# Cross-shaped window attention on one Trainium2 core: column heads staged in padded blocks, nine more tiles off ScalarE, the first x in quarters

## The chip, the cores and the metric

The kernel runs on one core of a Trainium2 chip. The metric is device time in microseconds (us) of the whole program, as the median of several runs; the profile is of one further execution. A core has TensorE (PE, matrix products, with weight loads listed apart as PEld), VectorE (DVE), ScalarE (ACT), GpSimd (POOL) and SyncE (SP), which here only issues transfers (DMA). PE writes to PSUM, eight banks of 512 floats in each of 128 partitions; all else lies in SBUF.

## The reference

An image of 224 x 224 tokens with 96 channels goes through one projection to q, k and v. The first 48 channels attend within stripes of 8 rows, the last 48 within stripes of 8 columns; both results, side by side, go through an output projection.

```python
qkv = jnp.einsum('bhwc,cd->bhwd', x, wqkv)          # x: (1, 224, 224, 96) bf16
q, k, v = qkv[..., :C], qkv[..., C:2*C], qkv[..., 2*C:]
scale = C2 ** (-0.5)                                 # C2 = 48, sw = 8
qh = q[..., :C2].reshape(B * nh, sw * W, C2)         # 28 row stripes of 1792 tokens; kh, vh alike
ah = _softmax(einsum('bqc,bkc->bqk', qh, kh) * scale)
oh = einsum('bqk,bkc->bqc', ah, vh).reshape(B, H, W, C2)
# qv, kv, vv: q, k, v [..., C2:] regrouped to 28 column stripes of 1792 tokens
av = _softmax(einsum('bqc,bkc->bqk', qv, kv) * scale)
ov = ...                                             # regrouped back to (B, H, W, C2)
return einsum('bhwc,cd->bhwd', concat(oh, ov), wo)
```

## The kernel before, in words

**Pairs and tiles.** Stripes are worked two at a time: pairs P = 0 to 13 (`NPH` = 14) are row stripes, pairs 14 to 27 column stripes. The two stripes of a pair (w = 0, 1) fill the two halves of PE's rows. Scores are computed transposed, keys by queries; the queries come in four chunks c (512, 512, 512, 256), the keys in 14 blocks of 128. A *tile* is one key block against 512 queries for both stripes, 128 x 1024 scores in two PSUM banks (in the last chunk two key blocks of 256 queries). A pair has 14 + 14 + 14 + 7 = 49 tiles.

**Who takes the exponential.** Most tiles go to ACT: one exponential, 128 x 1024, PSUM to the buffer `PT` (L859). The rest go to DVE and POOL, which approximate the exponential with squarings. Which ones is told by `KINDS` and, per pair, `KIND_OF`: a letter for each tile of a chunk that does not go to ACT. A tile of kind P is read by DVE (`p1`, L943, to `qb`), squared, scaled and squared again by POOL (L959, L960, L956), and PE computes its scores once more (L702) so that DVE adds the final factor (`f`, L948). A tile of kind R has a second DVE step (`p2`, L945) and one square on POOL. Kind 0 and kind 2 hold eight such tiles, kind 1 nine. Then the tile meets v on PE (L715), accumulating outputs and, in a 49th column, the sum of weights.

**The order.** Every engine's instructions are laid out when the program is built. `ORDER`, one string per pair, gives PE's order by hand: q is a score pass for ACT, v a product with v, 1 and 3 the first score pass of a DVE tile (in two halves or whole), 2 and 4 its second, k a projection of the next pair (keys `K`, queries `Q`, values `V`, one `fill` each), g a piece of the output projection, f a final piece of the last pair. A planner (`Sched`, `dve_step`, `pool_step`, the times `tm`, durations such as `D_H`, due times such as `TURN`) follows this order with modelled durations and so fixes the order on DVE, POOL and SP's queue. On the chip only semaphores decide; each engine takes its instructions in the fixed order.

**Getting x in.** The first pair's x comes in four transfers of 168 KB, two on SP's queue and two on ACT's (L287, `x_lead`), into memory that later belongs to `cat`; PE turns it (L737), DVE and ACT evict. Later pairs use transfers that turn (`DMA_TRANSPOSE`, L404), and the column stripes reread turned x from DRAM (`xt_dram`, `plan_x`).

**Getting the result out.** A finished chunk is copied to `OT_sb` (L876) and turned (`turn_ot`, L414); DVE takes reciprocals of the sums (`emit_rn`), POOL multiplies (`emit_norm`, L920). In the row half the result goes through `ohn` and copies (`keep_oh`) into `cat`, which holds for every token 96 channels: 48 of the row head, 48 of the column head. In the column half POOL writes the other 48 channels into `cat` directly. Then `turn_cat` turns a pair's part of `cat` in two pieces (`oc_T`, in `oc_all`); a block of 128 turned rows holds 1 1/3 blocks of 96 channels, so `wo6` keeps six shifted copies of wo, and some blocks need two matmuls (L637). DVE evicts five blocks at a time back into `cat` (L642), in place, after the pair's turns have read it (the keys `catd`), and each block of 128 tokens x 96 channels leaves as one store of 24 KB in runs of 192 bytes. The last pair's column head is projected without a turn (`fin_fills`, L602) and added (L614).

Of the kernel before, what the change touches and what calls it, by code (L numbers as in the profile page):

```python
# [20 lines left out]
KINDS = ["PPR PPR PP ", "PPR PRR PPR ", "PPR PPR PR "]  # L21
# [11 lines left out]
D_ST, D_SW, D_TAIL = 0.64, 1.3, 0.70  # L33
XR1, XR2, TURN = 19.5, 43.0, 4.5
D_H, D_F, D_SQ, D_AF = 0.604, 1.137, 1.9, 1.03
# [4 lines left out]
NTWICE = 11  # L40


KIND_OF = [0, 1, 1, 1, 1, 1, 1, 1, 1, 1, 1, 1, 1, 1, 2, 2, 2, 2, 2, 2, 2, 2, 2, 2, 2, 2, 2, 2]
ORDER = [
    "kkkqkq3qkq3qkkqkq1qkqq1q3qvkqv2qvkqv2qvqkkvqv1qkvqvkqvv2qvqv1qvvvqvkq2vqvkqkq1qkvvq2qvv2qvvq1vqkvqvvq1vqv2qvkvqvkvq",
    "1vqvvqvq2vvq3qvvvqvv3qqvqvvqkkkq2qvqvkvqv2qkvqv2qkvvvq1qvvvvqvqvv1qvvq2vq2qvkqvvq1vqvkq2vqv2qvvq1qvvqvkqvvkqkvqvkq2vvq2qvv3",
    "qvvqv1qvvq1vqvvqvvqv1qkq1qvvvqvq2qvkkqvqvk2qvvq3qvkqvkvq4qkqv1qvvq4qvkq2vqv1qvq4vqkq2vqv1qvvqvvqv2q1qvvqvkkqq1vkv",
    "qv2qvqv1qvvvqvvqv1qq1vvqvvqvvvq4qvkvq1vqvvqvq2vqv1qvv4qkqvv1qvqvkq2vqkvvq2vkqvkq3vqkqvvvqv1qvq4vqkq3vqkvq4vqvkvq4vqkvq2vk",
    "qvvq1vqvvvvqq2vvvqvvvq2vqvq14qvqkqv3qvkvqvvqvkqv1qkqvvq1vqvkq2vqvkq2qvvvq1qv1qkqvvvqkqvvkq2qvv3qkvqv3qvvqv4qvkqv4qkqvv1",
    "qvqvvvq2vqq1vvqvv1qvvqvqv2qq4vqvkq1vqvvvqvq1vqkvkqkvvq2kqv3qkvqv4qvvqkq1vqvvvqkqvv4qvqkv2qvvq2vqv1qvq4vqvvqkvkvq1qkvvq2v",  # L50
# [5 lines left out]
    "qvvq1vqvvqvq1vqv2qvvq1vqqvvvq1qkvvqvvqkvq4vqkvq1vkqv2qvq3qkvvq2kqvvq2qvv1qvqvvqv2qkvqv3qvkqv4qkqvv1qvvqkkqvkvq2qvvq2vvv",  # L56
    "q3qvvvqvvvqv1qvq2vvvqkq1vqvvq3qvvvqvvqvkq4qkvq1vkqq2vqv4qvkqv2qvvvq1vkqvkq4vqkqv2qvvvq1qvkqvvvq2qkqvvq1vvq2qvvkqkvq1vkq",
    "1qvvqvvq1qvv2qqvvq1vvqvqvv1qvqvqkvqv2qvkqv2qvvqk2qvkqv3qvkvq3qvvvq4qvkvq2qkvqkvq1vqvqkvvqvvq2vqvvq3qvvkq4vqkvqv2qvvq1vk",
    "qvq1vqvvqvvqv1qvv2qvvq1vqq2vqkvq1qvkqvvqvkvqv1qkvvq2qkvvq4vqvvkq1qvvvqvvqkqv4qkvqv4qkvvq1qvvq1vvvqv1qvqvvvvq4qvvvkq2qkvvqkvq2",
# [114 lines left out]
def bass_standalone__window_attn_cswin__vision_kernel(  # L174
# [28 lines left out]
    with es:  # L203
# [55 lines left out]
        for b in range(2):  # L259
            for w in range(2):  # L260
                SEMS[f"x{b}{w}"] = sem(f"s_x{b}{w}")
                SEMS[f"xp{b}{w}"] = sem(f"s_xp{b}{w}")
                SEMS[f"xr{b}{w}"] = sem(f"s_xr{b}{w}")
# [896 lines left out]
        def do_q():  # L1160
# [18 lines left out]
            if P not in begun:  # L1179
                begun.add(P)  # L1180
                p_t[P] = tm["end"]
                if ph_of(P):
                    tm["sp"] = max(tm["sp"], st) + 1.5
# [173 lines left out]
```

## Time and profile before

| what | value |
|---|---|
| time, median of 3 runs | 1062.62 us (1061.92 to 1063.65) |
| profiled execution | 1062.68 us, of which the span 1060.9 us from first to last instruction |
| busy in the span | PE 1033.4, DVE 998.2, ACT 1049.3, POOL 935.5 us |
| mean granted clock of TensorE | 0.999 |
| exponential tiles on ACT; tiles on DVE and POOL | 1135; 237 |
| matmuls of the output projection (L637) | 1176 |
| stores, 24 KB each | 392 |

The span is what the trace covers; the rest of the execution's own time lies around it. In a group's row, "x1135 | 1044.8, 1087" means 1135 instructions, 1044.8 us in which at least one of them ran, and 1087 ns for one; behind the second bar stands the engine's idle time ahead of them and what ended it.

### The profile page before, as it was taken

To read this page: it belongs to the slowest core of one execution; us is meant where nothing else is said; L and a number is where in the kernel's file an instruction comes from. 1 tells how busy PE (TensorE), PEld (TensorE's weight loads), DVE (VectorE), ACT (ScalarE), POOL (GpSimd) and SP (SyncE) were. 2 spreads that over 40 slices of the span, in tenths; PEclk is the share of its full clock that TensorE was granted. 3 is DMA by queue.
4 is the path that set the end of the run, shared out by engine and by line. 5 is a ranking of instruction groups with operands and counts; after the bars stand their busy time and mean duration, and the time that the engine had idled before them with its cause. 6 is when DMAs were issued, how large, how long until landed. Compare 5 with 4: busy or idle time off the path is not lost.

```text
span 1060.9 us, 33547 instructions
## 1 busy us (share of the span) xinstructions
PE 1033.4 (97%) x13812; PEld 393.5 (37%) x13812; DVE 998.2 (94%) x1720; ACT 1049.3 (99%) x1146; POOL 935.5 (88%) x617
## 2 busy tenths in 40 slices
PE   9999999999999999999999999999999999999998
PEld 4333333333333333333334433333343443344433
DVE  8999999999999999999999999999999999999988
ACT  8999999999999999999999999999999999999998
POOL 7999999999988989999999778888888878979784
PEclk9999999999999999999999999999999999999999
DMA  9987648754963874322115334423332342332342
GB/s 182 160 153 112 100 80 145 112 96 84 144 96 56 139 108 69 38 56 58 40 20 99 76 54 76 88 38 77 80 69 52 81 83 49 79 79 40 64 65 44
DMA packets 376217, 88.58 MB, mean 83 GB/s; under 512 B 366944, under 2 KB 373376, under 8 KB 376064
## 3 DMA queue, kind: packets, MB, share of 16 engines
q1 hardware_dynamic: 374816, 85.85, 46.8%
q8 instruction: 108, 1.77, 0.7%
q10 hardware_dynamic: 1120, 0.49, 0.2%
q14 instruction: 45, 0.37, 0.1%
q0 software_dynamic: 128, 0.10, 0.0%
HBM read 28.36 MB, written 28.21 MB: 53 GB/s over the span
## 4 chain that ended last, share of the span: by engine, by line
PE 54%; ACT 28%; DVE 7%; issue 6%; POOL 4%; DMA 0%; ACTq 0%; POOLq 0%; DVEq 0%
ACT PT L859 28%; PE ps L715 20%; PE ps L689 20%; PE ps L702 7%; PE ps L521 3%; DVE qb L943 2%; DVE PT L948 2%; PE ps L637 2%; POOL PT L959 2%; PE ps L566 1%; POOL PT L956 1%; POOL PT L960 1%; DVE PT L945 1%; DVE KT_sb L526 1%; POOL cat L920 0%
## 5 line engine op out<-in xcount | busy, mean ns | idle before, releaser
L859 ACT ACTIVATE PT<-ps 128x1024 bf16<-128x1024 f32 x1135 | 1044.8, 1087 | 2.8 <-PE ps L689 1.8
L689 PE MATMUL ps<-QT_sb,KT_sb 49*64 49x512 bf16 (+1 forms) x5368 | 465.3, 363 | 17.6 <-ACT PT L859 10.5
L956 POOL TENSOR_TENSOR PT<-PT 128x1024 f16<-128x1024 f16 x237 | 445.1, 1892 | 41.1 <-DVE PT L945 24.1
L715 PE MATMUL ps<-PT,V_sb 128*49 128x512 bf16 (+1 forms) x3136 | 464.7, 362 | 0.3
L948 DVE SCALAR_TENSOR_TENSOR PT<-ps,PT 128x512 uint16<-128x512 f32 (+1 forms) x398 | 302.0, 787 | 20.8 <-PE ps L702 13.5
L943 DVE TENSOR_SCALAR qb<-ps 128x512 f16<-128x512 int16 (+1 forms) x404 | 302.3, 778 | 20.3 <-PE ps L702 15.8
L959 POOL TENSOR_TENSOR PT<-qb 128x1024 f16<-128x1024 f16 x141 | 266.1, 1892 | 54.8 <-DVE qb L943 24.9
L689 PEld LDWEIGHTS ps<-QT_sb,KT_sb 49*64 49x64 bf16 x5368 | 136.4, 103 | 305.8 <-ACT PT L859 280.9
L715 PEld LDWEIGHTS ps<-PT,V_sb 128*49 128x49 bf16 x3136 | 134.8, 103 | 211.1 <-issue 181.4
L702 PE MATMUL ps<-QT_sb,KT_sb 53*64 53x512 bf16 (+1 forms) x1896 | 189.4, 389 | 4.0 <-DVE PT L948 0.7
L960 POOL TENSOR_SCALAR PT<-PT 128x1024 f16<-128x1024 f16 x141 | 147.1, 1043 | 12.0
L945 DVE SCALAR_TENSOR_TENSOR PT<-ps,qb 128x512 f16<-128x512 int16 (+1 forms) x166 | 122.5, 766 | 0.5
L702 PEld LDWEIGHTS ps<-QT_sb,KT_sb 53*64 53x64 bf16 (+1 forms) x1896 | 53.8, 104 | 71.2 <-DVE PT L948 21.7
L876 DVE CAST OT_sb<-ps 113x512 bf16<-113x512 f32 x112 | 69.1, 617 | 3.0 <-PE ps L715 2.7
L535 DVE CAST QT_sb<-ps 128x512 bf16<-128x512 f32 (+1 forms) x111 | 67.2, 616 | 2.5 <-PE ps L521 1.7
L526 DVE TENSOR_SCALAR_CACHE_REDUCE KT_sb<-ps 128x512 bf16<-128x512 f32 x108 | 65.4, 616 | 1.3 <-PE ps L521 0.6
L642 DVE CAST cat<-ps 128x480 bf16<-128x480 f32 x84 | 51.5, 617 | 5.1 <-PE ps L637 4.5
L573 DVE CAST V_sb<-ps 128x480 bf16<-128x480 f32 (+1 forms) x84 | 51.7, 620 | 1.5 <-PE ps L566 1.2
L521 PE MATMUL ps<-xT_sb,w_sb 97*64 97x512 bf16 (+1 forms) x224 | 40.7, 364 | 0.0
L521 PE MATMUL ps<-xT_sb,wq_sb 97*64 97x512 bf16 x224 | 40.5, 366 | 0.1
L637 PE MATMUL ps<-wo,oc_all 128*64 128x96 bf16 x1176 | 39.9, 208 | 0.0
L566 PEld LDWEIGHTS ps<-w_sb,xT_sb 96*64 96x64 bf16 x1568 | 33.1, 112 | 17.7 <-issue 7.4
(64 smaller groups left out, 254.7 us busy)
## 6 DMA issues: line engine op xcount, KB each, us to landing
xT_sb<-xt_dram SPq DMA_DIRECT2D x28, 336.0 KB, 4.0
out_dram<-cat SPq DMA_DIRECT2D x382, 24.0 KB, 1.9
xp_dram<-in_x_dram SPq DMA_DIRECT2D x26, 336.0 KB
oc_all<-xp_dram SPq DMA_DIRECT2D x26, 336.0 KB, 4.4
xt_dram<-xT_sb SPq DMA_DIRECT2D x26, 336.0 KB, 6.4
cat<-ohn SPq DMA_DIRECT2D x52, 84.0 KB, 3.2
xt_dram<-xT_sb SPq DMA_DIRECT2D x4, 168.0 KB, 5.3
OT_tr<-OT_sb SPq DMA_TRANSPOSE x40, 3.4
```

The lines of the kernel that those rows point to most:

```text
L521: ins = e.matmul(bk[64 * w:64 * w + 64, 0:qs], lhsT=lw, rhs=xT_sb[b][0:C + 1, w, q0:q0 + qs], start=True, stop=True)
L526: return e.tensor_scalar(KT_sb[b][:, q0:q0 + qs], bk[:, 0:qs], alpha, None, ALU.mult, ALU.add, accum_out=ksum[b][:, c:c + 1])
L689: ins = e.matmul(bank(SETS[s] + w)[64 * kh:64 * kh + 64, i * t["qs"]:(i + 1) * t["qs"]], lhsT=KT_sb[b][64 * w:64 * w + CA, kt * 128 + 64 * ...
L702: ins = e.matmul(bank(bp[w])[64 * kh:64 * kh + 64, 0:512], lhsT=KT_sb[b][64 * w:64 * w + nr, kt * 128 + 64 * kh:kt * 128 + 64 * kh + 64], ...
L715: ins = e.matmul(bank(pb)[64 * w:64 * w + CA, 0:t["qs"]], lhsT=V_sb[b][:, w, kt, :], rhs=PT[slot][:, ca:ca + t["qs"]], start=st and i == 0 ...
L859: S.commit("act", 0.0, D_ACT, None, lambda e, s=s, slot=slot: e.activation(PT[slot][:], ps[:, 512 * SETS[s]:512 * SETS[s] + 1024], ACTF.Ex ...
L943: fn, reads, writes = lambda e: e.tensor_scalar(q, l, m, a, ALU.mult, ALU.add), bk, qk
L945: fn, reads, writes = lambda e: e.scalar_tensor_tensor(y.bitcast(FP16), l, -RA * 2.0 ** 16, q, ALU.add, ALU.mult), bk + qk, ptk
L948: fn, reads, writes = lambda e: e.scalar_tensor_tensor(y.bitcast(U16), f, 128.0, y.bitcast(FP16), ALU.mult, ALU.add), bk + ptk, ptk
L956: square = ("pool", D_SQ, lambda e: e.tensor_tensor(y, y, y, ALU.mult), yk + ["pser"], yk)
L959: return [("pool", D_SQ, lambda e: e.tensor_tensor(y, q, q, ALU.mult), qk, yk), ("pool", D_AF, lambda e: e.tensor_scalar(y, y, -(QS * (RB ...
L960: ("pool", D_AF, lambda e: e.tensor_scalar(y, y, -(QS * (RB + RA) / 2) ** 2, 1.0, ALU.add, ALU.mult), yk + ["pser"], yk),
```

## The change

1. `KINDS` gets a fourth kind, PPR in three chunks (nine tiles: six P, three R). Nine of the 14 column pairs take it; five keep kind 2. `ORDER` is new for 23 of its 28 rows. It has letters for two fills with one common eviction (K, and G, of which no row makes use); K stands once.
2. `cat` goes. Row-head results lie in `oh_all`; for each column pair a copy (`rows_in`) brings its part into `stg`, where POOL also writes the column head. A block in `stg` is 96 channels and 32 zeros, so a turned block holds just one block of 96 channels, `wo6` shrinks to one copy, and each block takes one matmul per half. `stg` has two buffers: a turn waits for its own rows and its own half of the column head.
3. The eviction of the projection goes into `og` (two buffers and one for the last pair). One partition there holds two neighbouring tokens, so a store is 48 KB in runs of 384 bytes; there are half as many.
4. The last pair's row-head part is turned in two pieces, one after row pair 12 and one after 13, where both came after 13.
5. The first x comes in eight transfers of 84 KB, the four of h2 = 0 on SP's queue and the four of h2 = 1 on ACT's; the weights come third on SP's queue rather than after x.
6. The zeroing of `stg` stands among POOL's first instructions; two memsets for `cat` and `wo6` are gone. Modelled durations and due times of the planner change.

```diff
-KINDS = ["PPR PPR PP ", "PPR PRR PPR ", "PPR PPR PR "]
+KINDS = ["PPR PPR PP ", "PPR PRR PPR ", "PPR PPR PR ", "PPR PPR PPR "]
-KIND_OF = [0, 1, 1, 1, 1, 1, 1, 1, 1, 1, 1, 1, 1, 1, 2, 2, 2, 2, 2, 2, 2, 2, 2, 2, 2, 2, 2, 2]
+KIND_OF = [0, 1, 1, 1, 1, 1, 1, 1, 1, 1, 1, 1, 1, 1, 2, 3, 3, 3, 2, 3, 3, 3, 2, 3, 3, 3, 2, 2]
...
-D_ST, D_SW, D_TAIL = 0.64, 1.3, 0.70
+D_ST, D_SW, D_TAIL = 1.0, 0.60, 1.0
...
-        cat = sb("cat", [128, NPH, NPH, 2, C], BF16)
+        oh_all = sb("oh_all", [128, NPH, NPH, 2, C2], BF16)
+        stg = [sb(f"stg{i}", [128, NKT, 2, 128], BF16) for i in range(2)]
+        og = [sb(f"og{i}", [128, NKT // 2, 2, 2, C], BF16) for i in range(3)]
...
         for hf in range(2):
-            for w, q in ((0, "sp"), (1, "actq")):
-                dma(q, [], [("x", w, hf)], x0_sb[:, w, hf * FTH:(hf + 1) * FTH, :],
-                    x_lead[w][:, hf * FTH * C:(hf + 1) * FTH * C], f"x{w}{hf}", land=3.4 + 1.0 * hf + 0.3 * w)
-        dma("sp", [], ["wst"], wst[:, :], wqkv, "w0", land=5.2)
+            for w in range(2):
+                for h2, q in ((0, "sp"), (1, "actq")):
+                    k0 = hf * FTH + h2 * FQ
+                    dma(q, [], [("x", w, hf, h2)], x0_sb[:, w, k0:k0 + FQ, :],
+                        x_lead[w][:, k0 * C:(k0 + FQ) * C], f"x{w}{hf}{h2}", land=3.1 + 0.8 * hf + 0.4 * w + 0.2 * h2)
+            if hf == 0:
+                dma("sp", [], ["wst"], wst[:, :], wqkv, "w0", land=4.8)
...
-            pool_now([("cat", NPH - 1)], lambda e: e.memset(cat[:, NPH - 1, :, :, C2:C]...bitcast(FP32), 0.0), 0.7)
-            pool_now(["wo6z"], lambda e: e.memset(wo6[:]...bitcast(FP32), 0.0), 0.3)
+        pool_now([("stgz", 0)], lambda e: e.memset(stg[0][:, :, :, C:]...bitcast(FP32), 0.0), 0.5)
+        pool_now([("stgz", 1)], lambda e: e.memset(stg[1][:, :, :, :]...bitcast(FP32), 0.0), 1.8)
...
+        def rows_in(P, m0=0, m1=NPH):
+            b = P % 2
+            dma("sp", ["oh", ("stgz", b)], [("sr", b)], stg[b][:, m0:m1, :, 0:C2].rearrange("p m w c -> p (m w) c"),
+                oh_all[:, P - NPH, m0:m1, :, :].rearrange("p m w c -> p (m w) c"), f"ri{b}")
...
-            turn(f"oc{b}{z}", ["oh", ("cat", a), ("ov", a, z)], [("ocT", b, z), ("catd", a, z)] + x_old,
-                 oc_T[b][:, k0 * 2 * C // 128:k1 * 2 * C // 128, :], flat[:, k0 * 2 * C:k1 * 2 * C])
+            turn(f"oc{b}{z}", [("sr", b), ("sc", b, z), ("stgz", b)], [("ocT", b, z)],
+                 oc_T[b][:, 2 * k0:2 * k1, :], stg[b][:, k0:k1, :, :].rearrange("p m w c -> p (m w c)"), x_old)
...
-        dst_all = out[0].rearrange("(kt hh) (j dw) c -> j kt hh dw c", hh=16, dw=8)
+        dst_all = out[0].rearrange("(kp hh) (j dw) c -> j kp hh (dw c)", hh=32, dw=8)
...
                     for s in range(n):
-                        q, r = divmod(3 * (k0 + s), 4)
-                        use = {0: ((0, 0),), 3: ((0, 1), (1, 2)), 2: ((0, 3), (1, 4)), 1: ((0, 5),)}[r]
-                        for i, (dq_, v) in enumerate(use):
-                            for h in range(2):
-                                ins = e.matmul(bk[64 * h:64 * h + 64, s * C:(s + 1) * C], lhsT=oc_T[b][:, q + dq_, 64 * h:64 * h + 64],
-                                               rhs=wo6[:, v, :], start=i == 0, stop=i == len(use) - 1)
+                        m, u = divmod(k0 + s, 2)
+                        for h in range(2):
+                            ins = e.matmul(bk[64 * h:64 * h + 64, s * C:(s + 1) * C],
+                                           lhsT=oc_T[b][0:C, 4 * (m // 2) + 2 * h + m % 2, :].rearrange("c (t u) -> c u t", u=2)[:, u, :],
+                                           rhs=wo6[0:C, :], start=True, stop=True)
...
-                    tm["sp"] = max(tm["sp"], done) + (2.0 if z["z"] else 2.6)
+                    tm["sp"] = max(tm["sp"], done) + (2.3 if z["z"] else 3.1)
```

More of the change, by code (lines that the diff above doesn't have):

```diff
@@ L407, in turn_x, with turn @@
                 S.note(tok, reads, writes)
-        def turn(semn, reads, writes, out_ap, in_ap):
-            d = {k for k in S.deps("dma", reads, writes) if k[0] != semn}
+        def turn(semn, reads, writes, out_ap, in_ap, old=()):
+            d = {k for k in S.deps("dma", reads, writes + list(old)) if k[0] != semn}
             dma_tot[semn] += 16
```

219 lines of the change are left out of this document (152 added, 67 removed).

## The prediction

> **What bounds the kernel now.** I read the page first, then the busy time by stretches, then the list of waits, then the groups of instructions by shape, and last the two ends in the timeline. Busy shares and the groups of ScalarE (ACT), from the page:
>
> ```profile
> span 1060.9 us, 33547 instructions
> PE 1033.4 (97%) x13812; PEld 393.5 (37%) x13812; DVE 998.2 (94%) x1720; ACT 1049.3 (99%) x1146; POOL 935.5 (88%) x617
> L859 ACT ACTIVATE PT<-ps 128x1024 bf16<-128x1024 f32 x1135 | 1044.8, 1087 | 2.8 <-PE ps L689 1.8
> ```
>
> ACT is full: 1135 exponential tiles take 1044.8 us, one each 0.9205 us (instructions overlap, so the mean of one, 1087 ns, is longer), and only 2.8 us of idle time lie before them. The time is 1135 tiles, plus what comes before the first and after the last. TensorE (PE) looks nearly as full, but its largest waits, from the list of waits, are for ACT:
>
> ```profile
> PEld ps L689 <- ACT PT L859: 280.9, 803, 0.8
> ```
>
> Its weight loads stand 280.9 us behind ACT, so PE has room. The work is uneven between the halves; columns of the busy time by stretches are length, then busy time with count for each engine. The stretches are the first pair's head start, pairs 1 to 13, pairs 14 to 27, the densest single pairs for VectorE (DVE) and GpSimd (POOL), and the end.
>
> ```profile
> core 0: us, PE busy (x) PEld busy (x) DVE busy (x) ACT busy (x) POOL busy (x), PEclk, DMA share, GB/s
> 0.00:9.60 9.60, 8.23 (x74) 5.74 (x76) 5.36 (x30) 4.53 (x12) 6.83 (x22) 1.00 0.77 196
> 47.30:525.50 478.20, 465.14 (x5824) 167.22 (x5822) 460.44 (x773) 477.64 (x520) 445.39 (x293) 1.00 0.58 94
> 525.50:1053.00 527.50, 520.26 (x7350) 205.50 (x7340) 491.86 (x835) 526.68 (x574) 448.42 (x280) 1.00 0.35 67
> 231.20:268.00 36.80, 35.87 (x452) 12.51 (x446) 36.14 (x59) 36.80 (x41) 35.80 (x23) 1.00 0.62 105
> 415.10:451.90 36.80, 35.56 (x448) 12.47 (x448) 35.86 (x63) 36.80 (x41) 35.93 (x23) 1.00 0.52 73
> 1053.20:1060.90 7.70, 3.36 (x68) 2.12 (x68) 4.42 (x20) 2.77 (x4) 1.06 (x2) 0.85 0.28 57
> ```
>
> Pairs 1 to 13 already give DVE and POOL nine tiles each, and ACT stays full there (477.64 of 478.20 us) with DVE at 96.3% and POOL at 93.1%. Pairs 14 to 27 give them eight, and DVE stands at 93.2%, POOL at 85.0%. One pair has run with DVE at 98.2% (36.14 of 36.80), another with POOL at 97.6% (35.93), and in both ACT was busy throughout.
>
> **The change, part by part.**
>
> **Nine tiles leave ACT.** The old `KIND_OF` gives 14 pairs of the second half the kind with eight tiles off ACT; the new one gives nine of them a kind with nine ("PPR PPR PPR" against "PPR PPR PR "), so each of the nine gives one more tile, of kind P, to DVE and POOL. `ORDER` holds 1126 letters q against 1135. 9 x 0.9205 us = -8.3 us if nothing else stalls ACT. This is the main term.
>
> **What the nine tiles cost DVE.** In the letters of the second half, tiles read in two halves on their first visit (1) go from 70 to 78 and on their second (2) from 72 to 78; those read whole on the second visit (4) go from 40 to 44, and whole first visits (3) stay at 40. The timeline of DVE shows what one costs in a full queue, as the distance of starts:
>
> ```profile
> 236.56 1.89 DVE L943 TENSOR_SCALAR qb<-ps 128x512 f16<-128x512 int16 x3
> 238.37 1.28 DVE L945 SCALAR_TENSOR_TENSOR PT<-ps,qb 128x512 f16<-128x512 int16 x2
> 241.20 1.22 DVE L945 SCALAR_TENSOR_TENSOR PT<-ps,qb 128x1024 f16<-128x1024 int16 x1
> 242.33 0.68 DVE L526 TENSOR_SCALAR_CACHE_REDUCE KT_sb<-ps 128x512 bf16<-128x512 f32 x1
> ```
>
> Three halves start 1.81 us before the next instruction, 0.60 each; a whole tile 1.13. So 14 visits in halves x 1.21 and 4 whole x 1.13 add 21.4 us to DVE in the second half: 491.9 + 21.4 = 513.3, against 527.5 - 8.3 = 519.2 us of time, or 98.9%. At the share of the densest pair, 98.2%, the second half would need 513.3 / 0.982 = 522.7 us, 3.5 us more than ACT allows it. The bounds for this stall are 0 and, at the share of all of the first half, 96.3%, 513.3 / 0.963 = 533.0, or 13.8 us (that is a rival below). But busy time overstates a full queue: a half shows as 0.68 us when something waits behind it and takes 0.60 when the next one follows at once, so the share can grow without stalls as the queue fills. I take +1.8, halfway between 0 and 3.5. The one merged eviction (K, two chunks of keys in one instruction) is one instruction in the whole kernel and counts nothing.
>
> **What they cost POOL.** Rows of the page:
>
> ```profile
> L956 POOL TENSOR_TENSOR PT<-PT 128x1024 f16<-128x1024 f16 x237 | 445.1, 1892 | 41.1 <-DVE PT L945 24.1
> L959 POOL TENSOR_TENSOR PT<-qb 128x1024 f16<-128x1024 f16 x141 | 266.1, 1892 | 54.8 <-DVE qb L943 24.9
> L960 POOL TENSOR_SCALAR PT<-PT 128x1024 f16<-128x1024 f16 x141 | 147.1, 1043 | 12.0
> ```
>
> A tile of kind P is two squares and one scaling, 1.892 + 1.043 + 1.892 = 4.83 us. Nine add 43.4: 448.4 + 43.4 = 491.8 of 519.2 us, 94.7%, between the first half's 93.1% and the densest pair's 97.6%. So POOL fits on the whole; in one pair of nine tiles it is at 36 to 37 of 36.8 us, and every fourth pair has eight and lets it catch up. Nothing is added for it.
>
> The Trainium skill (SBUF — State Buffer, "Who interferes with whom") speaks against pressing these two together: DVE and GpSimd share a pair of SBUF ports, and a DVE instruction with two SBUF inputs or in a two-port mode blocks GpSimd for its whole length. The trace bounds that at nothing here: all 237 squares on POOL last between 1890 and 1895 ns while DVE is 94% busy:
>
> ```profile
> L956 POOL TENSOR_TENSOR PT<-PT x237: 1890/1892/1895, 18.9 to 1047.0; 128x1024 f16<-128x1024 f16 x119
> ```
>
> The change adds no new form beside POOL (the same reads of PSUM with at most one SBUF tile), so I add nothing.
>
> **The output projection.** The old turned layout needs 1176 matmuls at L637, because a block of 96 channels often straddles two turned columns; with 32 zeros behind each 96 channels (`stg`) one block is one column, and 14 pairs x 28 blocks x 2 halves = 784 remain.
>
> ```profile
> L637 PE MATMUL ps<-wo,oc_all 128*64 128x96 bf16 x1176 | 39.9, 208 | 0.0
> L637 PEld LDWEIGHTS ps<-wo,oc_all 128*64 128x64 bf16 x1176 | 31.9, 110 | 16.0 <-issue 6.2 <-DVE PT L948 1.7 <-DVE qb L943 1.1
> L702 PE MATMUL ps<-QT_sb,KT_sb 53*64 53x512 bf16 x948 | 94.8, 390 | 1.8 <-DVE PT L948 0.5 <-DVE OT_sb L876 0.2 <-DVE wq_sb L552 0.2
> ```
>
> 392 x 34 ns = 13.3 us less PE work; the nine tiles add a second score pass of 4 matmuls at 0.1 us each, 3.6 us. PE in the second half goes from 520.3 to about 510.6 of 519.2 us: the same share, with the same wait for ACT as cover. The new loads read every second token. No load in this trace is strided, so I bound it between no change and twice the 27 ns of a load (31.9 / 1176), 784 x 27 ns = 21 us of weight loading. That would eat the PE saving but lies under the 280.9 us of waits for ACT, so 0 on the path either way.
>
> **Stores, staging and turns on SP's queue.** From the issues of transfers and the waits of SP:
>
> ```profile
> out_dram<-cat SPq DMA_DIRECT2D x382, 24.0 KB, 1.9
> oc_all<-cat SPq DMA_TRANSPOSE x28, 3.7
> cat<-ohn SPq DMA_DIRECT2D x52, 84.0 KB, 3.2
> xt_dram<-xT_sb SPq DMA_DIRECT2D x26, 336.0 KB, 6.4
> SPq L287 <- DVE cat L642: 72.2, 28, 7.1
> ```
>
> 392 stores of 24 KB become 196 of 48 KB; SP stands 72.2 us waiting for their evictions, so they are not late now and take fewer places in the queue. Added is a copy of 336 KB in 96-byte runs per pair (`rows_in`), for which the nearest rows are 3.2 us for a quarter of it and 6.4 us for a copy as large in 128-byte runs. It is issued at the pair's start and needed some half a pair (18 us) later, which hides it; if it came late, a turn would wait behind it, and so would the stores and `plan_x` loads queued after it. The turns carry 4/3 as many blocks: 3.7 us becomes at most 4.9. Their readers are the g fills, which `ORDER` lists later in time and which PE meets in order. I take 0, and keep the upper end as a rival.
>
> **POOL's memsets** for `stg` (2.4 us, at the rate of a 128x448 one in 0.47 us) move to the start; the old start has POOL done at 9.5 us and its first tile at 12.6 us, which covers them. 0.
>
> **The first x as eight quarters.** The timeline of the start and its transfers:
>
> ```profile
> 0.74 0.89 SPq L287 DMA_DIRECT2D cat<-in_x_dram  x2
> 0.75 0.91 ACTq L287 DMA_DIRECT2D cat<-in_x_dram  x2
> 3.04 0.47 POOL L342 MEMSET oc_all<- 128x448 f32 x1
> 8.83 0.69 POOL L362 MEMSET wqT<- 128x256 bf16 x2
> 3.99 3.22 PE L737 MATMUL ps<-ident,cat 112*96 112x112 bf16 x32 [0.33 <-DMA cat<-in_x_dram]
> 5.01 0.54 ACT L753 ACTIVATE xT_sb<-ps 96x448 bf16<-96x448 bf16 x1 [1.81 <-PE ps L737]
> 11.44 1.22 DVE L943 TENSOR_SCALAR qb<-ps 128x1024 f16<-128x1024 int16 x1
> cat<-in_x_dram SPq DMA_DIRECT2D x2, 168.0 KB, 3.5
> cat<-ohn SPq DMA_DIRECT2D x8, 42.0 KB, 2.2
> ```
>
> The first transposes start when 168 KB have landed, 3.5 us after the issue; 42 KB of another copy land in 2.2. An 84 KB quarter lands in between, so a gain of up to 1.3 us, and a loss of up to 0.9 us because each queue issues four transfers instead of two (0.45 us each) and ACT's table load and first eviction are queued behind them. ACT sits idle 1.81 us before that eviction, which covers the 0.9. After the first quarters the chain of evictions runs at the same pace, and the later ones still wait for the same bytes. I take -0.3.
>
> **The end.** The last stretch, 7.7 us, keeps its chain (last tile, eviction, projection, store) with half the stores; but row 27 of `ORDER` now carries ten g fills instead of seven. I take 0, between -0.5 (one issue of a transfer, 0.45) and +1.8 (three evictions at the 0.60 of a half).
>
> **Sum**, against the profiled execution's 1062.68 us: -8.3 + 1.8 - 0.3 = -6.8, **1055.9 us**; the median of the runs, 1062.62, lies 0.06 under it, so the same to 0.1 us.
>
> **The rivals.**
>
> *DVE cannot fill up* (slower). For it: the shares of busy time never passed 96.3% over a whole half. Then the second half takes 533.0 us, +13.8, and -8.3 + 13.8 - 0.3 gives 1067.9. It decides from a sustained ceiling of 513.3 / 527.5 = 97.3%: below that the nine tiles cost more than ACT saves. Against it: the 98.2% pair, and the 0.08 us of every lone instruction that vanish in a full queue. 0.14.
>
> *POOL is the bound.* If its share cannot pass the first half's 93.1%, 491.8 / 0.931 = 528.2, +9.0: 1063.4, no change. Against it: two pairs above 97% with ACT full, and 41.1 and 54.8 us of idle time before its squares that are waits for input, not gaps. 0.09.
>
> *The turns come late.* 28 turns, each 1.2 us longer, of which the new due times in the diff (2.3 and 3.1 for 2.0 and 2.6) grant 0.3 to 0.5: 28 x 0.8 = 22 us if PE met every one unprepared and ACT had no tile in hand, so -8.3 - 0.3 + 22 = 1076. Against it: fewer stores before each turn. 0.05.
>
> *It gains all it can:* no stall at all and the full head start, -8.3 - 1.3: 1053.1, with the shorter end 1052.5. It belongs to the forecast's own range.
>
> **How the numbers follow.** The forecast's case, ACT still the bound with a stall between none and 6 us, has 0.72 and its own range is 1052 to 1060.4. What a measurement of this kernel can tell from no change is 0.2%, 2.1 us. Of the forecast's case nearly all is faster by more than that; 0.02 lies within. Faster 0.70, same 0.02 + the POOL rival's 0.09 + a thin edge of the DVE rival = 0.12, slower the rest, 0.18. The range reaches from the full gain, 1051.5, over the POOL rival to 1063.5; about 0.2 lies outside, mostly above.
>
> **What would show it.** Right: 1126 activations at 0.92 us each, idle before them under 6 us; 784 matmuls in place of 1176; DVE and POOL in the second half at 97 to 99% and about 95%. Wrong: ten or more microseconds of idle time before ACT's tiles, ended by PE passes that themselves waited for DVE or POOL (the first two rivals) or for a turn's transfer (the third); a first activation later than 9.6 us would refute the head start.

## The result, and the profile after

The changed kernel takes **1058.24 us** (median of 6 runs, 1056.43 to 1059.63) against 1062.34 us before (6 runs beside it, 1061.92 to 1063.65): a ratio of 0.9959, 95% interval 0.9944 to 0.9973. It is faster, by 4.1 us instead of the forecast 6.8. The runs fall into two groups, which matters below: 1056.43, 1056.43 and 1057.32 at a mean granted clock of 0.999 to 1.0, and 1059.17, 1059.55 and 1059.63 at 0.997 to 0.998. The profiled execution is one of the fastest, 1056.43 us.

The page of the profile after, in the order of the rows shown of before: span, busy shares, ScalarE's exponential (now L872), POOL's squares (now L1007), and the second scores on PE (L715), which DVE reads.

```profile
span 1054.6 us, 32763 instructions
PE 1025.1 (97%) x13456; PEld 384.5 (36%) x13456; DVE 1013.5 (96%) x1748; ACT 1041.5 (99%) x1137; POOL 985.2 (93%) x654
L872 ACT ACTIVATE PT<-ps 128x1024 bf16<-128x1024 f32 x1126 | 1037.1, 1080 | 3.9 <-PE ps L702 2.8
L1007 POOL TENSOR_TENSOR PT<-PT 128x1024 f16<-128x1024 f16 x246 | 461.9, 1894 | 20.0 <-DVE PT L996 11.2
L715 PE MATMUL ps<-QT_sb,KT_sb 50*64 50x512 bf16 (+1 forms) x1968 | 196.7, 390 | 6.3 <-DVE KT_sb L540 1.2
```

ACT still bounds the kernel: 1126 tiles, 3.9 us idle before them. The busy time by stretches (pairs 1 to 13 with the first, pairs 14 to 27, the end; columns as before) shows that the second half is now as full as the first:

```profile
core 0: us, PE busy (x) PEld busy (x) DVE busy (x) ACT busy (x) POOL busy (x), PEclk, DMA share, GB/s
8.80:524.80 516.00, 502.87 (x6348) 178.90 (x6341) 497.33 (x831) 515.65 (x562) 484.51 (x317) 1.00 0.53 100
524.80:1046.50 521.70, 511.93 (x6986) 198.69 (x6986) 506.23 (x866) 519.25 (x564) 489.61 (x309) 1.00 0.54 83
1046.50:1054.60 8.10, 3.17 (x64) 2.00 (x62) 4.79 (x24) 2.24 (x3) 4.41 (x9) 0.89 0.29 82
```

DVE is at 506.23 of 521.70 us, 97.0%, POOL at 93.8%. But ACT, which missed 0.8 us of the second half before (526.68 of 527.50), now misses 2.45. That is the first thing to explain. The second is the end, for which the groups of instructions by shape give the first and last start of ACT's tiles, before and after:

```profile
L859 ACT ACTIVATE PT<-ps x1135: 1018/1081/1276, 9.6 to 1054.9; 128x1024 bf16<-128x1024 f32 x190
```
```profile
L872 ACT ACTIVATE PT<-ps x1126: 1017/1071/1265, 8.8 to 1047.7; 128x1024 bf16<-128x1024 f32 x188
```

| us | before | after | difference |
|---|---|---|---|
| start to the first tile | 9.6 | 8.8 | -0.8 |
| first to last tile | 1045.3 | 1038.9 | -6.4 |
| last tile's start to the end of the span | 6.0 | 6.9 | +0.9 |

So in this execution 6.4 of the forecast 8.3 us arrived between the tiles, and the end lost 0.9.

**Where ACT waits.** The list of waits names one that the kernel before did not have:

```profile
PEld ps L702 <- ACT PT L872: 284.3, 815, 0.8
DVE rn L956 <- DMA OT_tr<-OT_sb: 1.2, 1, 1.2
```

Only one wait, 1.2 us. The timeline at that place (start, length; SP's issues first) shows what follows from it:

```profile
564.66 0.60 SPq L292 DMA_DIRECT2D stg<-oh_all  x1
565.30 3.00 SPq L292 DMA_DIRECT2D xT_sb<-xt_dram  x2
568.40 1.24 SPq L423 DMA_TRANSPOSE OT_tr<-OT_sb  x1
575.29 0.23 DVE L956 RECIPROCAL rn<-OT_tr 128x12 f32<-128x12 bf16 x1 [1.19 <-DMA OT_tr<-OT_sb]
575.44 0.36 DVE L540 TENSOR_SCALAR_CACHE_REDUCE KT_sb<-ps 128x256 bf16<-128x256 f32 x1
575.87 0.41 PE L715 MATMUL ps<-QT_sb,KT_sb 50*64 50x512 bf16 x4 [1.18 <-DVE KT_sb L540]
576.54 3.77 ACT L872 ACTIVATE PT<-ps 128x1024 bf16<-128x1024 f32 x4 [1.05 <-PE ps L702]
```

SP issues the new copy for the turns (`rows_in`) at the start of pair 15, behind it the loads of the next x (336 KB each), and only then the second turn of pair 14's result, `OT_tr`. That turn lands 6.9 us after its issue (568.40 to 575.29; the median of the 40 is 4.2). DVE takes its instructions in order: the reciprocal L956 that reads the turn stands for 1.19 us, behind it the eviction of K (L540), behind that PE's second score pass (L715), and with PE the tiles of ACT, which idles 1.05 us. That is 1.05 of the 2.45 us that ACT misses in this half. The transfers themselves became slower too (columns: count, size, median us from issue to landing; the two turns took 3.4 and 3.7 us before, the second with three quarters of the blocks):

```profile
stg<-oh_all SPq DMA_DIRECT2D x13, 336.0 KB, 6.0
OT_tr<-OT_sb SPq DMA_TRANSPOSE x40, 4.2
oc_all<-stg SPq DMA_TRANSPOSE x28, 4.6
```

The theory taken into the experiments: the late turn makes the stall, and PE's idle time then costs clock. Its rivals: DVE is simply full (the prediction's own term), or the new layout or the quarters cost something by themselves.

### The profile page after: what moved, and what is told of

Same layout as the page of the kernel before. It is cut to its first block, busy times and chain, and to the rows that moved or that the text cites. A ratio compares the mean times of both kernels' runs of the same rounds, so it can differ in the third digit from the quotient of the medians.

```text
span 1054.6 us, 32763 instructions
## 1 busy us (share of the span) xinstructions
PE 1025.1 (97%) x13456; PEld 384.5 (36%) x13456; DVE 1013.5 (96%) x1748; ACT 1041.5 (99%) x1137; POOL 985.2 (93%) x654
## 4 chain that ended last, share of the span: by engine, by line
PE 55%; ACT 23%; DVE 10%; issue 6%; POOL 5%; DMA 1%; ACTq 0%; SPq 0%; POOLq 0%; DVEq 0%
ACT PT L872 23%; PE ps L728 21%; PE ps L702 21%; PE ps L715 8%; PE ps L535 3%; DVE qb L994 3%; DVE PT L999 3%; POOL PT L1007 2%; POOL PT L1010 2%; PE ps L580 1%; PE ps L649 1%; DVE PT L996 1%; POOL PT L1011 1%; DMA OT_tr<-OT_sb 1%; DVE OT_sb L889 1%
## 5 line engine op out<-in xcount | busy, mean ns | idle before, releaser
L872 ACT ACTIVATE PT<-ps 128x1024 bf16<-128x1024 f32 x1126 | 1037.1, 1080 | 3.9 <-PE ps L702 2.8
L1007 POOL TENSOR_TENSOR PT<-PT 128x1024 f16<-128x1024 f16 x246 | 461.9, 1894 | 20.0 <-DVE PT L996 11.2
L999 DVE SCALAR_TENSOR_TENSOR PT<-ps,PT 128x512 uint16<-128x512 f32 (+1 forms) x405 | 312.3, 800 | 14.9 <-PE ps L715 6.6
L994 DVE TENSOR_SCALAR qb<-ps 128x512 f16<-128x512 int16 (+1 forms) x421 | 313.6, 775 | 12.2 <-PE ps L715 7.3
L1010 POOL TENSOR_TENSOR PT<-qb 128x1024 f16<-128x1024 f16 x150 | 283.3, 1894 | 22.9 <-DVE qb L994 9.4
L715 PE MATMUL ps<-QT_sb,KT_sb 50*64 50x512 bf16 (+1 forms) x1968 | 196.7, 390 | 6.3 <-DVE KT_sb L540 1.2
L1011 POOL TENSOR_SCALAR PT<-PT 128x1024 f16<-128x1024 f16 x150 | 156.9, 1046 | 12.8
L715 PEld LDWEIGHTS ps<-QT_sb,KT_sb 50*64 50x64 bf16 (+1 forms) x1968 | 55.8, 103 | 77.0 <-DVE PT L999 22.3
L540 DVE TENSOR_SCALAR_CACHE_REDUCE KT_sb<-ps 128x512 bf16<-128x512 f32 x106 | 63.7, 616 | 1.3 <-PE ps L535 0.8
L655 DVE CAST og<-ps 128x480 bf16<-128x480 f32 x84 | 51.3, 616 | 1.4 <-PE ps L649 0.8
L535 PE MATMUL ps<-xT_sb,w_sb 97*64 97x512 bf16 x224 | 40.7, 365 | 0.3 <-DVE qb L994 0.2
L580 PE MATMUL ps<-w_sb,xT_sb 96*64 96x48 bf16 x1568 | 39.1, 190 | 0.0
```

Of the source, the lines that this page charges most:

```text
L535: ins = e.matmul(bk[64 * w:64 * w + 64, 0:qs], lhsT=lw, rhs=xT_sb[b][0:C + 1, w, q0:q0 + qs], start=True, stop=True)
L580: ins = e.matmul(bk[64 * h:64 * h + 64, j * C2:(j + 1) * C2], lhsT=xT_sb[b][0:C, w, t0:t0 + 64], rhs=w_sb[0:C, wblk(P, "v"), 0:C2], start= ...
L715: ins = e.matmul(bank(bp[w])[64 * kh:64 * kh + 64, 0:512], lhsT=KT_sb[b][64 * w:64 * w + nr, kt * 128 + 64 * kh:kt * 128 + 64 * kh + 64], ...
L872: S.commit("act", 0.0, D_ACT, None, lambda e, s=s, slot=slot: e.activation(PT[slot][:], ps[:, 512 * SETS[s]:512 * SETS[s] + 1024], ACTF.Ex ...
L994: fn, reads, writes = lambda e: e.tensor_scalar(q, l, m, a, ALU.mult, ALU.add), bk, qk
L999: fn, reads, writes = lambda e: e.scalar_tensor_tensor(y.bitcast(U16), f, 128.0, y.bitcast(FP16), ALU.mult, ALU.add), bk + ptk, ptk
```

## The experiments

**The parts.** Four kernels: the change as it is; with x in halves; the new layout with the old `KIND_OF` and `ORDER`; the old layout with the new ones.

```diff
 e1: -for w, for (h2, q): eight transfers of 84 KB
     +for (w, q): four transfers of 168 KB, weights last, as before
 e2: -KIND_OF, ORDER of the change      +KIND_OF, ORDER of before
 e3 (from before): -KIND_OF, ORDER of before   +KINDS, KIND_OF, ORDER of the change
```

> The changed kernel unchanged, as the base for the runs beside it and to see whether its stalls lie at the same places. Theory (a transfer that comes late): the stall of about 2 us near 574 us, where DVE waited 1.19 us for the second turn of pair 14's result, stands in every execution with another length, and the time lies between 1056.4 and 1059.6 us as the length varies. Rival (DVE is too full): the stalls are the same in every execution, since the instruction order is fixed, and the idle time before ACT's tiles is again 3.9 us within 0.3.

> The changed kernel with the first x in four transfers of 168 KB as before. Theory (the quarters are worth the whole shift of the first activation, 9.57 to 8.82 us): first activation back at 9.5 to 9.6 us and the time 0.75 us above the changed kernel run beside it. Rival (the shift is taken up later, since the first P tiles on POOL set the pace to about 20 us): first activation at 9.6 us but the time within 0.3 us of the changed kernel.

> The changed kernel with KIND_OF and ORDER of before: staging, stores and quarters, but 1135 tiles on ACT. Theory (late transfers): the copies to the staging buffer are still there, so about 1 us of stall and the 0.9 us of the longer end stand against the 0.75 us of the head start: 1062.5 to 1064. Rival (DVE fullness): no stall beyond those of before, so -0.75 + 0.9 = 1062.3 to 1062.7. If the layout saved time by itself: under 1061.

> The kernel before with KIND_OF and ORDER of the changed kernel (its one K written as kk): 1126 tiles on ACT in the old layout, x in halves. Theory (the tiles are the gain and the layout only costs): -8.3 and the stalls of full queues, 1055 to 1058. Rival (the layout is what lets the tiles gain): the output projection has 392 more matmuls, g comes earlier in the order than the old turns can deliver, and the time is 1060 to 1066 with ACT's idle time above 8 us.

Measured on one chip, before at 1062.44 (17 runs):

| | median us (range, runs) | ratio [95%] |
|---|---|---|
| e0, the change again | 1057.11 (1055.73 to 1057.6, 5) | 0.9943 [0.9931, 0.9956] |
| e1, x in halves | 1057.86 (1055.1 to 1061.45, 6) | 0.9956 [0.994, 0.9972] |
| e2, layout only | 1063.44 (1063.21 to 1064.3, 11) | 1.0009 [1.0001, 1.0018] |
| e3, tiles only | 1075.4 (1073.25 to 1077.62, 4) | 1.012 [1.0107, 1.0133] |

The layout by itself brings nothing (+1.0, of which the first tile at 10.4 instead of 9.6 us is most), as the prediction's "0 on the path" for PE's saving said: PE had the room. The time of e2 lies in the range that I gave for late transfers, but its trace has no wait of DVE for the turn, so that was luck. The gain comes with the nine tiles and their order, but only with the layout: on the old one the same order loses 13 us, and its 1075.4 lies above both of my ranges for e3. Where it loses them, from the page and the waits of e3:

```profile
L859 ACT ACTIVATE PT<-ps 128x1024 bf16<-128x1024 f32 x1126 | 1041.1, 1068 | 14.4 <-PE ps L689 12.7
```
```profile
ACT PT L859 <- PE ps L689: 12.7, 17, 5.5
PEld ps L637 <- DMA oc_all<-cat: 4.4, 1, 4.4
```

ACT waits for PE, up to 5.5 us at a stretch, and PE once 4.4 us for a turned result. This order was laid out for fewer stores and the new layout's turns, so e3 says that the two belong together, not what nine tiles would cost in an order made for the old layout. DVE does the same tiles in e3 as in e0, so it is not DVE alone.

e1 did not settle the quarters: three of its executions had a clock of 0.999 or more and took 1055.1 to 1057.2 us, three had 0.996 to 0.998 and took 1058.6 to 1061.5. All five of e0 had at least 0.999. The first tile in the profile of e1 came at 8.7 us, with halves, where I had expected 9.5 to 9.6 or more.

e0 and e1 also contradict my theory of a stall in every execution. Their queue has the copy in the same place as the changed kernel, and in neither trace does DVE wait for the turn. SP's issue and DVE's reciprocal in e0, by the timeline:

```profile
568.88 1.24 SPq L423 DMA_TRANSPOSE OT_tr<-OT_sb  x1
575.63 0.22 DVE L956 RECIPROCAL rn<-OT_tr 128x12 f32<-128x12 bf16 x1
```

Here the turn landed 5.4 us after its issue instead of 6.9, and DVE came to it only after that. ACT's idle time of 4.1 us before its tiles is the rival's 3.9 within 0.3 in number only: 2.1 of it stand before the first tile, against 1.1 in the changed kernel's profile.

**The late turn, DVE, and the end.** Three edits of the changed kernel and the quarters put into the kernel before.

```diff
 e4, at the start of pair P:            -            if P > NPH:
                                        -                rows_in(P)
     behind turn_ot(P, c // 2):         +            if c == 3 and P + 1 < NP - 1:
                                        +                rows_in(P + 1)
 e5, eviction of the projection: -tensor_copy(rows[:, k0:k0 + n, :], ...)
                                 +tensor_copy(rows[:, k0:k0 + n, 0:C2], ...[:, :, 0:C2])
 e6: -D_ST, D_SW, D_TAIL = 1.0, 0.60, 1.0     +D_ST, D_SW, D_TAIL = 1.0, 1.30, 1.0
 e7 (from before): the first x as eight quarters, weights third
```

e5 leaves out half of the projection's eviction: 48 of the 96 channels are copied, and the staging buffers hold some x there instead.

> The changed kernel with the copy to the staging buffer (rows_in) of pair P+1 issued right behind the second turn of pair P's result, instead of ahead of it at the start of pair P+1; the order on all other engines is the same. Theory (the copy makes that turn land late, 6.8 us near 574 us where 4.2 is the median; DVE waits, PE idles, and in some executions TensorE loses its full clock for one or two stretches of 3.4 us): the turn of the first such pair lands in about 4 us, no stall over 1 us near 574 us, no execution with a mean clock under 0.999, and the times lie within 1055 to 1058 us, median 1056.5. Rival (the low clocks have another cause): mean clocks of 0.996 to 0.998 appear again in one of three executions and the median stays at 1057 to 1058.

> The changed kernel with the 84 evictions of the output projection copying only the first 48 of 96 channels (the other half of og is filled once from x, and the output is wrong there): it takes some 84 x 0.24 = 20 us off DVE in the second half, as much as the nine tiles added. Theory (what the body gives back, 7.3 of 8.3 us arriving, is DVE being too full in single pairs): idle before ACT's tiles and the small gaps fall, 1 to 2 us faster than the changed kernel, pairs 17 and 26 without their 0.6 us. Rival (order and late transfers, not fullness): within 0.5 us.

> The changed kernel with the planner's cost of a store from POOL's queue back at 1.30 (it was set to 0.60): 8 of the 14 late stores move from POOL's queue to SP's and ACT's; nothing else moves. Theory (the end is 0.9 us longer because the last two stores queue behind each other on POOL, each 0.55 us, and land 2.6 us after their issue): the stretch from ACT's last tile to the end falls from 6.96 to 6.0 to 6.4 us and the time by 0.6 to 0.9. Rival (the end is set by the last pair's evictions on DVE): 6.8 to 7.0 us, no change.

> The kernel before with only the first x in eight transfers of 84 KB. Theory (the first activation is set by when TensorE gets its full clock, which it got between 4.4 and 9.8 us after the start in six traces, and not by the transfers): within 0.3 us of the kernel before, 1062.2 to 1062.8; the first activation lies at 8.7 to 10.4 us depending on that moment alone. Rival (the quarters gain the 0.75 us seen in the profile): 1061.5 to 1061.9.

Measured on another chip, before at 1062.60 (26 runs):

| | median us (range, runs) | ratio [95%] |
|---|---|---|
| e4, copy behind the turn | 1056.46 (1054.99 to 1063.31, 6) | 0.9948 [0.9928, 0.9968] |
| e5, narrow evictions | 1060.86 (1059.25 to 1066.25, 8) | 0.9985 [0.9972, 0.9998] |
| e6, the end's queues | 1058.85 (1055.18 to 1066.81, 12) | 0.997 [0.9957, 0.9984] |
| e7, quarters only | 1063.69 (1062.15 to 1064.46, 11) | 1.0007 [0.9998, 1.0015] |

e5 was to be 1 to 2 us faster if DVE was too full. Its time cannot tell, because all eight executions had a clock of 0.996 to 0.998, but its trace can. DVE is busy 999.1 us in it, against 1013.5 in the changed kernel. ACT idles 8.3 us before its tiles, of which 2.1 stand before the first and 4.4 at and behind the late turn; 1.8 remain. In the changed kernel the same sum is 3.9 - 1.1 - 1.05, also 1.8. So 14 us less work on DVE took nothing off ACT's other idle time. The busy time of e5 by stretches of 3.41 us around the late turn (here the reciprocal waited 1.80 us) shows where its time went:

```profile
573.24:576.65 3.41, 3.40 (x36) 0.96 (x32) 2.69 (x6) 3.41 (x5) 3.41 (x3) 1.00 0.65 132
576.65:580.07 3.42, 1.63 (x22) 0.54 (x22) 2.20 (x7) 1.69 (x3) 3.13 (x3) 1.00 0.00 0
580.07:583.48 3.41, 3.35 (x28) 1.09 (x26) 2.67 (x5) 2.51 (x4) 3.33 (x3) 0.50 0.82 154
```

In the stretch with the late turn PE was busy for 1.63 us of 3.42. In the next one the granted clock is 0.50 (the third column from the end), PE is "busy" for nearly all of it with 28 matmuls (a mean stretch of the changed kernel's second half has 46), and ACT gets 2.51 us of work. A stall of 1.8 us thus costs ACT 1.7 us in its own stretch and 0.9 in the next, and the trace has one more at half clock after it. The same pattern stands twice in e3, whose clock fell at 63.80 us and for two stretches at 565.56:

```profile
60.39:63.80 3.41, 2.12 (x26) 0.63 (x22) 1.15 (x2) 3.19 (x4) 3.41 (x3) 1.00 1.44 177
63.80:67.21 3.41, 3.41 (x22) 0.64 (x20) 2.46 (x5) 1.72 (x2) 3.33 (x3) 0.50 0.70 149
67.21:70.60 3.39, 3.39 (x36) 1.12 (x34) 3.19 (x6) 3.14 (x5) 3.31 (x3) 1.00 1.37 181
```

Here 2.12 us of busy PE in a stretch did not keep the clock. In the profiled execution of the changed kernel itself the stall lay across the edge of two such stretches (counted in steps of 3.41 us from where its trace first shows the full clock, 4.87 us):

```profile
571.48:574.89 3.41, 3.20 (x36) 0.96 (x32) 2.50 (x5) 3.41 (x5) 3.41 (x3) 1.00 0.57 117
574.89:578.30 3.41, 2.37 (x30) 0.78 (x30) 3.01 (x9) 2.36 (x3) 3.41 (x3) 1.00 0.06 11
```

2.37 us were enough, and the clock stayed. So a stall of little over a microsecond loses the clock or keeps it by where it falls in the 3.41 us. That would explain the two groups of times of the same kernel, but it is not shown for them: no execution of the slower group was profiled.

e4 takes the cause away. Its reciprocal waits for no turn, and four of its six executions take 1054.99 to 1056.68 us at 0.999 or more; one at 0.998 took 1056.66, and one of 1063.31 us at 0.999 has no explanation here. The one at 0.998 is the profiled one: its clock is full from 10.3 to 1051.4 us and halves only for the end, so a mean of 0.998 does not by itself mean that the clock fell on the way. e6 has the old stall (0.82 us in its trace) and eleven of its twelve executions are at 0.996 to 0.998; its one profile at 1.0 took 1055.18. Counted at 0.997 or less, on this one chip, they are eight of twelve in e6 and six of eight in e5, with the copy in front, and none of six in e4, with the copy behind.

e7: quarters in the kernel before cost 1.1 us between the medians, with an interval that touches 1. A gain of 0.3 is not what it shows, and neither of my two ranges for it came.

**All together, and one step back.** e8 has the copy of e4 and the due time of e6; e9 is e8 with x in halves; e10 is e8 with three more idle matmuls between the first two quarters' transposes and the last two (modelled landing `3.1 + 2.2 * hf` for `3.1 + 0.8 * hf`); e11 is e10 with the copy back at the start of the pair.

> Both earlier edits together: the copy for the turns is issued behind the last turn of the pair before, and the last stores are given 1.30 us of due time instead of 0.60. Theory (a late second turn of pair 14 stalls PE, and PE's idle time then drops the clock): no stall over 1.5 us in pair 15, mean clock 0.999 or more in nearly all executions, an end of about 6.1 us instead of 7.0, and so 1055.0 to 1056.5 us with a spread under 3 us. Rival (the clock falls for a reason of its own, with any order): clocks of 0.996 to 0.998 in half of the executions and a median of 1057.5 to 1059.

> The kernel of the run beside it (copy behind the turn, 1.30 us for the last stores), with the first x in four halves as in the kernel before. Theory (the quarters make the arrival of the full clock in the head a toss between about 4.5 and 10 us): the first tile before 9.6 us more often than with quarters, and a median 0.3 to 1 us lower than the run beside it, 1054.5 to 1055.5. Rival (the onset does not depend on how x is cut): the same median within 0.3 us, and the same two values of the first tile.

> The same as the first of these three, quarters kept, but 0.6 us of idle matmuls (one of 512 columns and two of 128 more) stand between the first two quarters' transposes and the last two, where TensorE otherwise has nothing to do for 0.3 to 0.5 us. Theory (that gap spoils the first busy window): the full clock by about 5.3 us, transposes at about 1 us for 16, the first tile at 8.8 to 9.0 us in the profile, and a median about 0.5 to 1 us under the first run. Rival (the phase of the window alone decides): nothing changes, or up to 0.3 us is lost when the filling stands in front of a quarter that has landed.

> The fastest kernel so far (due time of the last stores 1.30, filled gap in the head, copy behind the turn) with one edit taken back: the copy for the turns stands at the start of its pair again. Theory (the copy holds up the loads and the second turn of pair 14, PE idles, the clock drops): mean clocks under 0.999 in a third or more of the executions, those at 1057 us or more, the others at 1054.5 to 1055.5; in the profile the second turn of pair 14 is issued 2 us after its pair's copy and the interval after it is short of ACT work or at half clock when it drops. Rival (the drops belonged to the chip or the hour of the earlier runs, not to the copy): no clock under 0.999 and a median within 0.5 us of 1054.3.

| | median us (range, runs) | before beside it | ratio [95%] |
|---|---|---|---|
| e8 | 1054.62 (1054.55 to 1056.2, 5) | 1062.36 (9) | 0.9928 [0.9916, 0.9941] |
| e9, halves | 1055.03 (1054.62 to 1055.77, 5) | 1062.36 | 0.9928 [0.9916, 0.9941] |
| e10, gap filled | 1054.32 (1054.18 to 1054.89, 5) | 1062.36 | 0.9921 [0.9908, 0.9935] |
| e11, copy put back | 1055.75 (1054.8 to 1056.24, 5) | 1062.99 (9) | 0.9929 [0.9916, 0.9943] |

The median of e8 lies 0.4 us below the range that I gave, with the clocks as expected. None of the fifteen executions of e8 to e10 has a clock under 0.999, against eleven of twelve in e6, which differs from e8 by the copy alone (on another chip). e10 is the fastest version, 8.0 us under before. SP's queue and DVE's reciprocals in e8, by the timeline:

```profile
562.08 1.15 SPq L292 DMA_DIRECT2D xT_sb<-xt_dram  x2
566.30 1.23 SPq L423 DMA_TRANSPOSE OT_tr<-OT_sb  x1
567.58 0.62 SPq L292 DMA_DIRECT2D stg<-oh_all  x1
570.40 0.24 DVE L956 RECIPROCAL rn<-OT_tr 128x16 f32<-128x16 bf16 x1
574.40 0.22 DVE L956 RECIPROCAL rn<-OT_tr 128x12 f32<-128x12 bf16 x1
```

With the copy behind it, the loads go out at 562.08 instead of 565.30 and the turn at 566.30 instead of 568.40, and no reciprocal waits. The page of e8 has ACT's idle time back at what it was before the change:

```profile
L872 ACT ACTIVATE PT<-ps 128x1024 bf16<-128x1024 f32 x1126 | 1037.1, 1081 | 2.8 <-PE ps L702 1.6
```

In the second half (524.80 to 1044.90 us) ACT then misses 1.3 us, against 2.45 in the changed kernel and 0.8 before.

e11, on a third chip, brings the stall back but not the fall of the clock. The timeline of its DVE, and the stretch around it (of its steps of 3.41 us):

```profile
576.01 0.23 DVE L956 RECIPROCAL rn<-OT_tr 128x12 f32<-128x12 bf16 x1 [1.08 <-DMA OT_tr<-OT_sb]
```
```profile
573.88:577.29 3.41, 2.34 (x34) 0.71 (x26) 2.23 (x7) 2.40 (x4) 3.41 (x3) 1.00 0.00 0
```

My expectation of clocks under 0.999 in a third of its runs was wrong: the clock stayed, with 2.34 us of busy PE in the worst stretch. From the first to the last tile its trace takes 1038.7 us where that of e10 takes 1037.3. Its median is 7.2 us under its own before, where e10 is 8.0 under; with intervals that overlap, this difference alone would not show the stall. The traces side by side do:

| trace | copy | turn, issue to landing, us | DVE waits, us | first to last tile, us |
|---|---|---|---|---|
| the change | in front | 6.9 | 1.19 | 1038.9 |
| e5 | in front | 7.5 | 1.80 | 1041.9 |
| e6 | in front | 6.9 | 0.82 | 1038.3 |
| e11 | in front | 6.8 | 1.08 | 1038.7 |
| e0, e1 | in front | 5.4, 5.5 | 0 | 1038.0, 1037.7 |
| e4, e8, e9, e10 | behind | 2.7 to 2.8 | 0 | 1037.3 to 1037.6 |

So the place of the copy decides how long the turn takes to land. With the copy in front the turn comes late in four traces of six, behind it in none of four. The fall of the clock comes on top in some executions. What sets how often, between none of five (e0, e11) and eleven of twelve (e6), is open beyond the length of the stall and its phase; chip and head differ between these runs.

**The head.** e9 and e10 were to settle the quarters. What sets the first tile is not the landing of x but when PE comes to the full clock, which the durations in the timeline of PE show. The change in its profile, then e0, the same kernel (16 transposes L750, then two matmuls of 512 columns):

```profile
5.47 0.96 PE L750 MATMUL ps<-ident,oh_all 112*96 112x112 bf16 x16 [0.47 <-DMA oh_all<-in_x_dram]
6.36 0.41 PE L535 MATMUL ps<-xT_sb,wq_sb 97*64 97x512 bf16 x2
```
```profile
5.32 1.70 PE L750 MATMUL ps<-ident,oh_all 112*96 112x112 bf16 x16 [0.31 <-DVE xT_sb L762]
6.95 0.64 PE L535 MATMUL ps<-xT_sb,wq_sb 97*64 97x512 bf16 x2
```

0.96 against 1.70 us for the same 16 transposes: full and half clock, by the same instructions in the same order. The first tile came at 8.8 and 10.4 us. e9, with halves, was at half clock until 9.1 us (its two matmuls took 0.64 us, its first tile came at 10.2), so the halves are no cure, and my expectation for it fell: its median is 0.4 us above e8, not below. In all 14 traces the first tile follows the full clock, with quarters and halves alike: full clock at 4.4 to 5.2 us and first tile at 8.7 to 9.1 (five traces, e1 with halves), at 6.6 to 7.4 and 9.5 to 9.7 (three), at 9.1 to 10.3 and 10.2 to 10.6 (six). e10 had neither of the two onsets that were seen with quarters: half clock in the first 16 transposes, the change within the last 16 (1.40 us), the first tile at 9.5, in five executions within 0.7 us of each other:

```profile
3.27 1.73 PE L750 MATMUL ps<-ident,oh_all 112*96 112x112 bf16 x16
4.93 0.85 PE L377 MATMUL ps<-warm 128*64 128x512 bf16 x3
5.71 1.40 PE L750 MATMUL ps<-ident,oh_all 112*96 112x112 bf16 x16
7.04 0.41 PE L535 MATMUL ps<-xT_sb,wq_sb 97*64 97x512 bf16 x2
```

The 8.8 to 9.0 us that I expected did not come; a median 0.3 us under that of e8 is too little to tell apart with five runs each.

## Why the prediction was right or wrong

- **Nine tiles off ACT, -8.3:** right in kind and nearly in size. From the first to the last tile e8 and e10 need 1037.6 and 1037.3 us against 1045.3, so 7.7 to 8.0 of it arrive when nothing else is in the way.
- **DVE's fullness, +1.8:** the wrong cause. The second half of the changed kernel ran DVE at 97.0%, above the 96.3% of the ceiling rival, and e8 does so with ACT idle for 2.8 us, what it was before the change. Busy time grew by 14.4 us (491.86 to 506.23), not by 21.4: as the prediction noted, a lone instruction shows longer than it costs in a full queue, and this was a larger part than I allowed. Added up one by one from the two traces, the instructions of this half grow by 20.8 us, and 6.3 us more of them overlap. At most 0.3 to 0.6 us, what e8 and e10 lack of 8.3, can be DVE's. The rival "DVE cannot fill up" is refuted by the same rows, and e5's trace agrees: less work on DVE freed no time on ACT. That the profiled execution came within 0.1 us of the forecast between the tiles (-6.4 against -8.3 + 1.8) is luck: the late turn took what I had set aside for DVE.
- **POOL fits, +0:** right; 93.8% in the second half, its squares at 1894 ns against 1892.
- **The projection, 0:** right. 784 matmuls (x13456 in all for x13812) are busy for 31.8 us instead of 39.9, so they save PE 8.1 us and not the 13.3 of the working; the strided loads at a median of 110 ns as the plain ones before, and the layout alone saves no time (e2).
- **Stores, staging and turns, 0:** the step that failed. I wrote that the copy is issued at the pair's start and that its length hides it, and named what would be behind it if it came late: a turn. But it needs not be late itself. The loads of x and the second turn of the pair before stand behind it on SP's queue whatever it does; the turn then landed 6.9 us after its issue in the profile, and DVE, PE and ACT wait behind one reciprocal. I priced the turns by their lengths (1.2 us more each) and did not walk the queue at the place where the copy goes in. Price: about 1.1 us in the profile, nothing in e0 and e1, where the turn landed in time, and 4.4 us of ACT's time in e5, where the clock fell with it. The profiled execution, 1056.43, is 0.5 us above the forecast. The other 1.8 us up to the median of 1058.24 come with the three executions at a clock of 0.997 to 0.998; that the late turn made them slow fits the counts of e4 and e6, but none of them was profiled.
- **The quarters, -0.3:** the head start was argued from transfers, and what counts is the clock. With the gap between the quarters' transposes the full clock came early in some executions and late in others; in the kernel before the median is 1.1 us higher with them (e7, the interval touches 1). The profiled first tile at 8.8 us looked like the full gain, and was the lucky case: e1 has its first tile at 8.7 us with halves.
- **The end, 0:** +0.9 in the profile, within the bound of 1.8, but not by evictions. The due times put the last stores on POOL's queue one behind the other, by its timeline:

```profile
1050.72 0.55 POOL L292 DMA_DIRECT2D out_dram<-og  x1 [0.67 <-DVE og L628]
1051.46 1.09 POOL L292 DMA_DIRECT2D out_dram<-og  x2 [0.19 <-DVE og L628]
```

  Two issues of 0.55 us in a row there; with 1.30 us of due time (e6, e8) ACT's queue takes four of the last stores from POOL's and 6.1 us remain from the last tile to the end, against 6.0 before the change.
- **The rivals:** POOL's bound and the late turns as priced (every turn late, 1076) did not come. (POOL's sum left out the quarters: with their -0.3 it gives 1063.1, not 1063.4; and the range begins 1 us below the full gain as worked out, 1052.5.) One turn of 40 was late; the mechanism that I gave 0.05 was there in one place.

## What to carry to other kernels

When a transfer is put into a queue, list what stands behind it at that place and follow the latest of these to the engine that waits, instruction by instruction; whether the transfer itself has time to spare says little. A stall on the engine that feeds the bound is worth more than its length where it can cost clock: look for two groups of times and a mean clock a few thousandths lower before looking for a mechanism that is always there. And test a "full engine" by giving it less to do, and read the trace and not only the time: here the run was slower for another reason, but the idle time that the full engine was to explain had not shrunk. Last, profile one execution of each group: a single profile showed a stall that two others of the same queue order did not have.

## What the runs showed of the hardware

The granted clock changes in steps of 3.41 us. A stretch in which PE was busy for 1.63 or 2.12 of its 3.41 us was followed by one at half clock, one with 2.28 (e8, 4.56 to 7.97 us), 2.34 or 2.37 was not. So 1.1 us of idle PE in a stretch were let pass here, and 1.3 us was too much; a stall of 1.2 to 1.8 us can do either, by where it falls. The Trainium skill (TensorE: Matmul & The Clock Gate, Part 1) states the window, 3413 ns, free-running, and the trace agrees; the same page (Why this matters for your kernels) warns of idle gaps of more than about 3 us between bursts, where here less than 2 us of idle time in one window was enough. How much PE counts as busy is modelled in the profile, so the limit between 2.12 and 2.28 us is one of its readings.

At the start the full clock came, by the trace's clock records, at 4.9 us in the changed kernel, 9.8 in e0, 9.1 in e9 and 6.6 in e10. All four fit a window of 3.41 us that ends there and in which PE had no gap of 0.3 us or more; in e0 the window before it holds the gap of 0.31 us shown above. The other ten traces fit too: no gap in the window that ends at the full clock is over 0.24 us. That is a reading of the traces, with e10 as the one run that was made for it, and it came out at neither of the two values that I had expected.
